# FNet mixing and one-token expert layer: stores moved from ScalarE to GpSimd, the sum behind the scores pushed ahead, and the second DFT of two pairs placed before the second group's sequence products

## The chip, the cores and the metric

The kernel runs on one core of a Trainium2 chip. The metric is the device time of one execution in microseconds. Five engines work side by side, each with its own queue of instructions in a fixed order: TensorE (PE in the profile; PEld is its loading of weights), VectorE (DVE), ScalarE (ACT), GpSimd (POOL) and SyncE (SP), which here only issues DMAs. An instruction at the head of a queue that waits holds everything behind it. ScalarE and GpSimd can issue DMAs, too, from the same queue in which their computing stands.

## The reference

With x of 2048 tokens by 576 features in fp32:

```python
a = einsum("bsd,ed->bse", LN(x), dft_hid_re)
b = einsum("bsd,ed->bse", LN(x), dft_hid_im)
h = x + einsum("ts,bse->bte", dft_seq_re, a) - einsum("ts,bse->bte", dft_seq_im, b)

n = LN(h)
r = n @ w_r                                  # one score per token
idx = argsort(-r)[:, :1]                     # the best token alone
g = silu(n[idx] @ w_gate); u = n[idx] @ w_up # 576 -> 4608
y = ((g * u) @ w_down) * sigmoid(r[idx])     # 4608 -> 576
out = h + n + scatter(y at idx)
```

All of the DFT matrices come as inputs, and so do the three weights of 4608 x 576, of which every byte is read for a single token.

## The kernel before

**Layout.** A token is p * 16 + k, with p the partition and k one of 16 slots, so X is a tile of 128 partitions by 16 rows of 576 features (and one column of padding). Slots k and 16 - k form a pair (1 to 7); 0 and 8 stand alone. In the code, `FOLDED` is the list of these nine, and `GROUPS` splits them into group 0 (pairs 1 to 5, ten rows of X) and group 1 (pairs 6 and 7, and 0 and 8, six rows).

**Stages.** The rows are loaded and folded by symmetry (`fold_d`, `fold`, `folded`) into XF. `seq(g, n)` are the products of the sequence matrix with XF for group g, five of them (n = 0 to 4) per group; `keep` copies their result out of PSUM, one half through ScalarE (L538) and one through VectorE (L542), into Z. `hid(g, c)` is the second DFT, over the features, of the c-th pair of group g: TensorE takes Z and the matrices WA, WB and WC (L569) and leaves `py`, to which VectorE adds the rows of X (`residual`, L577) and the totals (`totals`, L582). `seq` of group 1 overwrites nothing that `hid` of group 0 reads, but `keep` of group 1 writes into the same Z, and so waits for it.

**Scores, results, stores.** `spread_of` (ScalarE, L587) measures each row's variance, `root` (L221) takes the root of a batch (`BATCHES`: pairs 1 to 3, pairs 4 and 5, 6 and 7, then 0 and 8), `scores` (VectorE, L593 to 603) makes the scores R and the factors of a batch, `result` (ScalarE, L608) makes the output of one row in place, and `store` writes rows out: slots below 9 in runs (`STORE_RUNS`, (1, 3) is slots 1 to 3 in one DMA) from ScalarE's queue, the others by one indirect DMA each from GpSimd's. `scores` reads wsum, the sum of the router's weights, which `sum_wr` (L886, L887) makes from wr.

**Checks.** The kernel uses symmetries of the given matrices and proves them as it goes: mirrored blocks are fetched by indirect DMAs from GpSimd (`load_c` and `gather`, L278), VectorE subtracts or adds them (`off_s` L353, `off_t` L358, `off_h` L365, `off_w` L420 to 425) into one of two halves of Q, and ScalarE squares and sums these (L346). If the sum weren't zero a general program behind the kernel would run instead. The direct loads of the matrix are SP's (L335). A buffer of the matrix (D0, D1, D2 and seven raw ones) comes free when its checks and products are done.

**The token.** `argmax` finds the best score over all tokens (VectorE and TensorE in turn), `row_of_token` (L960) fetches its row of X, `to_all` (L966, L967) spreads it over the partitions, `normalized` (L974) writes it to PSUM as `xsp`, and `copy_xs` (ScalarE, L979) copies it to SBUF. The last three wait for all results.

**The expert layer.** The three weights come as 54 tiles of 576 KB by SP (`load_ffn`, L1052) into 33 places: whatever the stages before leave free (XF, Z, Q, WA, WB, WC, the D tiles and the raw ones), and each place again once its tile is used. Gate and up tiles are multiplied with the token's row and summed by VectorE (`products`, L1061, reading PSUM), or multiplied by GpSimd (L1072) or VectorE (L1068) and summed by ScalarE (L1077); `gated` (L1086 to 1089) makes H, `down` (L1097) multiplies with the down tiles on TensorE, and `last_store` (L1112) writes the token's row over what was stored.

**What sets the order.** Each step is entered with `add(engine, duration, function, *dependencies, tail=, push=)` into a `Plan`, and `Plan.order` lists them: engine by engine it takes, among the steps that are open at that time, the one with the largest remaining way to the end plus its push. That list is the order of the program, so each engine runs its steps in it. `EARLY` gives the spreads, roots, scores, results and stores of group 0 a push of 300. TensorE's steps are chained by `pe_last` in the order in which they are entered, so the loops that enter `seq_step` and `hid_step` write its order out by hand:

```python
for n in (0, 1):
    seq_step(1, n)
for c in range(len(GROUPS[0])):
    hid_step(0, c)
for n in (0, 1):
    keep_step(1, n)
for n in (2, 3, 4):
    seq_step(1, n)
```

The waits of the chip are set by what each instruction reads and writes, not by the plan; two engines that read the same PSUM tile also wait for each other in program order.

Of the kernel before, what the change touches and what calls it, by code (L numbers as in the profile page):

```python
# [16 lines left out]
D = 576  # L17
# [21 lines left out]
GROUPS = [[1, 2, 3, 4, 5], [6, 7, 0, 8]]  # L39
# [27 lines left out]
class Plan:  # L67
# [6 lines left out]
    def add(self, eng, dur, fn, *deps, tail=0.0, push=0.0):  # L74
        flat = []
        for d in deps:
            flat += d if isinstance(d, list) else [d]
        n = {"eng": eng, "dur": dur, "fn": fn, "deps": [d for d in flat if d], "tail": tail, "push": push}
        n["i"] = len(self.ops)
        self.ops.append(n)  # L80
        return n
# [54 lines left out]
def kernel(  # L136
# [13 lines left out]
    pe, act, dve, pool, sp = nc.tensor, nc.scalar, nc.vector, nc.gpsimd, nc.sync  # L150
# [121 lines left out]
    ov = out.rearrange("(p k) d -> p k d", k=NK)  # L272
# [9 lines left out]
    X = mp.tile([P, NK, XW], F32, name="X")  # L282
# [272 lines left out]
    def slots_of(j):  # L555
        return [j, NK - j] if j in PAIRS else [j]

    def cols(t, js):

        n0 = POS[js[0]]  # L560
        return t[:, n0 : n0 + sum(len(slots_of(j)) for j in js)]
# [49 lines left out]

    def store(k, m):
        if k < 9:
            st = act.dma_start(ov[:, k : k + m, :], X[:, k : k + m, 0:D])
        else:
            n = POS[k]
            st = pool.indirect_dma_start(  # L617
                out, bass.IndirectOffsetOnAxis(ap=ti[:, n : n + 1], axis=0), X[:, k, 0:D], None
            )

        for group in ("spread",) if k < 9 else ("spread", "direct"):
            tc.declare_no_dep(st.ins, group=group, reason="stores of different rows")
        tc.add_to_no_dep_group("direct" if k < 9 else "spread", st.ins)
        if k >= 9:
            pool.memset(tick, 0.0)

    tick = mp.tile([1, 1], F32, name="tick")
    junk2 = mp.tile([P, D], BF16, name="junk2")
# [3 lines left out]
    add = plan.add  # L632

    def then(f, *args):
        return lambda: f(*args)
# [20 lines left out]
    def in_turn(eng, f, mb, *deps):  # L656
        LAST[eng], d = load(eng, f, mb, LAST[eng], *deps)
        return d
# [11 lines left out]
    w0 = in_turn("SP", lambda: sp.dma_start(wr, w_r.unsqueeze(0).to_broadcast([P, D])), 0.295)  # L670
    MEAS, DOTX, DFOLD = {}, {}, {}
    for a, b in X_RUNS:
# [3 lines left out]
        m = [add("ACT", 0.95, then(measure, k), DFOLD[k]) for k in ks]  # L676
# [15 lines left out]
    for k in FOLDED:  # L692
        dg, use, at = [], [], []
        for sl in slots_of(k):
            n = next(places)
            UF[sl] = LATER[n]
            at.append(PLACE[n])
            if k in PAIRS:
                u, w = dgs.take()
# [50 lines left out]
    def c_half(j):  # L750
        u, w = qs.take()
        n = [add("DVE", 0.93, then(off_h, j, i, u), CU[j, i, False][1], w) for i in range(2)]
        for i in range(2):
            users[CU[j, i, False][0]].append(n[i])
        squares(u, 9 * P, n)

    def squares(u, w, n, ps=P):
        SQUARES.append(add("ACT", 0.3 + w / 1200, then(square, u, w, ps), n))
        qs.users[u].append(SQUARES[-1])
# [54 lines left out]
    RESULTS = []  # L814
# [28 lines left out]
    def hid_step(g, c):  # L843
        nonlocal pe_last
        j = GROUPS[g][c]
        (y0, w0_), (y1, w1_) = ys.take(), ys.take()
        pe_last = add("PE", 0.99, then(hid, g, c, [0]), KEPT[g], WRAP, w0_, w1_, pe_last)
        ZU.setdefault((g, False), []).append(pe_last)
        pe_last = add("PE", 4 * 0.99, then(hid, g, c, [1, 2, 3, 4]), pe_last)
        ZU.setdefault((g, True), []).append(pe_last)  # L850
        users["Z"] = [pe_last]
        for b in ("WA", "WB", "WC"):
            users[b] = [pe_last] + WS
        ks = slots_of(j)
        res = [add("DVE", 0.72, then(residual, j, k), pe_last, DOTX[k]) for k in ks]
        m = add("DVE", 0.2, then(totals, j), pe_last, [d for k in ks for d in DOTX[k]])
        ys.users[y0] += res + [m]
        ys.users[y1] += res + [m]
        RES[j] = [add("ACT", 0.9, then(spread_of, k), m, r, push=EARLY[g]) for k, r in zip(ks, res)]
        for js in BATCHES:  # L860
            if j == js[-1]:
                batch(js)

    def batch(js):
        push = EARLY[js[0] in GROUPS[1]]
        v = add(
            "ACT", 0.3, then(root, cols(SD, js), cols(VAR, js), UNIT), [n for j in js for n in RES[j]], push=push
        )
        f = add("DVE", 1.85, then(scores, js), v, ws, push=push)
        SCORES.append(f)  # L870
        for k in [k for j in js for k in slots_of(j)]:
            RESULTS.append(add("ACT", 0.86, then(result, k), f, push=push))
            if k > 8:
                o = add("POOL", 1.3, then(store, k, 1), RESULTS[-1], push=push)
                STORES.append(add("DMA", 0.8, None, o, tail=2.0, push=push))
        for k, n in STORE_RUNS:
            if k in js:
                o = add("ACT", 0.35, then(store, k, n), RESULTS, push=push)
                STORES.append(add("DMA", 0.76 * n, None, o, tail=2.0, push=push))

    EARLY = (300.0, 0.0)
# [4 lines left out]
        dve.tensor_reduce(wsum[:, 0:1], wr, axis=AX.X, op=OP.add)  # L886
        dve.tensor_scalar(wsum[:, 1:2], wsum[:, 0:1], -1.0 / D, None, op0=OP.mult)  # L887

    ws = add("DVE", 0.9, sum_wr, w0)
    def no_more(tag):  # L890
        for b in [b for b in free if type(b) is tuple and b[0] == tag]:
            free.remove(b)
# [23 lines left out]
            c_check(j, i)  # L916
    for j in GROUPS[1]:
        c_half(j)
    for n in (0, 1):
        seq_step(1, n)  # L920
    for c in range(len(GROUPS[0])):
        hid_step(0, c)
    for n in (0, 1):
        keep_step(1, n)
# [73 lines left out]
    xs_is = add("DVE", 1.2, normalized, step)  # L998
    xs_on = add("ACT", 0.7, copy_xs, xs_is)
# [23 lines left out]
    o = add("DVE", 1.0, check_sum, SCORES, SQUARES, xs_is)  # L1023
    o = add("PE", 0.3, check_all, o)
# [4 lines left out]
    for b in range(NJ // 4):  # L1029
        j = 4 * b  # L1030
# [92 lines left out]
    def plan_ffn(after):  # L1123

        del plan.ops[base[0] :]
        del moved[base[1] :]
        del in_flight["SP"][base[3] :]
        LAST["SP"], last = base[2], None
        plan.order()
        at = {b: over(ns) for b, ns in users.items()}  # L1130
        used = dict(users)
        came, done, where, got = {}, {}, {}, {}

        def load_to(n):

            while len(came) < min(n, len(FT)):
                b = min((b for b in at if used[b]), key=lambda b: at[b])
                w, j = FT[len(came)]
                w_, came[w, j] = load("SP", then(load_ffn, b, w, j), 0.59, used[b], LAST["SP"])
                LAST["SP"] = w_  # L1140
                used[b] = done[w, j] = []
                at[b] = after.get((w, j), 1e3 + len(came))

        def products_of(w, j):
            c = came[w, j]
            b = j // 4
            if j % 4 == 0 and b < 8 and (w == "u" or b % 2):
                o = add("POOL", 2.65, then(products_on_pool, w, j), c, xs_on)
                o = add("ACT", 1.75, then(sums, w, j), o)
            elif j % 4 == 0 and b < 8:  # L1150
                o = add("DVE", 1.36, then(products_only, w, j), c, xs_is)
                o = add("ACT", 1.75, then(sums, w, j), o)
            else:
                o = add("DVE", 1.68, then(products, w, j), c, xs_is)
            done[w, j].append(o)
            got[w, j] = o

        def gate_and_down(j0, j1):
            nonlocal last
            js = slice(j0, j1)  # L1160
            o = add("ACT", 0.3, then(gated, js, 0), [got["g", j] for j in range(j0, j1, JW)])
            o = add("DVE", 0.5, then(gated, js, 1), o, [got["u", j] for j in range(j0, j1, JW)])
            for j in range(j0, j1, JW):
                last = add("PE", 1.0, then(down, j), came["d", j], o, last)
                done["d", j].append(last)

        load_to(N_BUF)
        for b in range(NJ // 4):
            j = 4 * b
            if b < NJ // 4 - 1:  # L1170
                for w in "gu":
                    for r in (0, JW):
                        products_of(w, j + r)
                gate_and_down(j, j + 4)
            else:
                for r in (0, JW):
                    for w in "gu":
                        products_of(w, j + r)
                    gate_and_down(j + r, j + r + JW)
            load_to(N_BUF + 6 * (b + 1))  # L1180
        o = add("DVE", 0.8, last_of_row, last, row1)
        end = add("SP", 1.0, last_store, o, STORES, LAST["SP"])
        todo = plan.order()
        return end["end"], todo, {t: over(ns) for t, ns in done.items()}
# [14 lines left out]
    with tc.If(mv):  # L1199
        with ExitStack() as gen:  # L1200
# [29 lines left out]
            with ExitStack() as hs:  # L1230
# [4 lines left out]
                for k in range(NK):  # L1235
# [3 lines left out]
                    for a in range(5):  # L1239
                        w = min(P, D - a * P)  # L1240
# [3 lines left out]
                    for c in range(4):  # L1244
                        pa = zbank(f"gpa{k}_{c}")
                        for a in range(5):
                            w = min(P, D - a * P)
# [29 lines left out]
            c, ci = steps[4]()  # L1277
# [80 lines left out]
```

## Time and profile before

| | |
|---|---|
| median of 3 runs | 226.23 us (225.82 to 227.1) |
| profiled execution, device time | 224.98 us |
| profiled execution, span of the instructions | 223.3 us |
| mean granted TensorE clock | 0.855 |
| moved by DMA | 78.12 MB, 73.16 read and 4.72 written in HBM |
| busy: VectorE, ScalarE, TensorE, GpSimd | 178.4, 146.5, 135.7, 107.4 us |

Times in the profile are microseconds from the start of the span. A row of the timeline gives the start, the length, the engine, the line in the kernel, the operation, the tiles written and read with partitions x elements, and in brackets how long the engine had been idle before and what it waited for. A row of the waits reads: who waited <- for whom: us in total, times, the longest. A row of a page's groups ends in busy us, mean ns of one, and the idle time before. "SPq", "ACTq" are the queues in which DMAs are issued.

### The profile page before, as it was taken

Reading aid. Unit: us, or ns where it says so; the run is one execution under the profiler, and the core shown is the slowest. Engines: PE = TensorE matmul, PEld = TensorE weight load, DVE = VectorE, ACT = ScalarE, POOL = GpSimd, SP = SyncE. Lnnn points to the kernel's source line nnn. Section 1 sums busy time; section 2 is a strip of 40 time slices with the busy share of each in tenths; the row PEclk is TensorE's granted clock in tenths of the full one; section 3 lists DMA queues with packets and bytes.
Section 4 is the critical chain, followed back from the end, with each engine's and each line's share of the span. In section 5 each row is a group of like instructions: output and inputs, shape, how many; then the busy total and the mean of one; then the engine's idle time right before and its main releaser. Section 6 shows DMA issues by size and latency. Waiting matters only on the chain.

```text
span 223.3 us, 2563 instructions
## 1 busy us (share of the span) xinstructions
PE 135.7 (61%) x606; PEld 87.9 (39%) x606; DVE 178.4 (80%) x466; ACT 146.5 (66%) x288; POOL 107.4 (48%) x96
## 2 busy tenths in 40 slices
PE   0009879999900899999999999011400475565150
PEld 0006547755600687777876776000200121121010
DVE  6587988999999729799989999987415997978810
ACT  3386997599684077878558489999407898683000
POOL 7727897456468810258810000076005999990000
PEclk9999999999995699999999999655555599799755
DMA  6999999999899999799989999999999999999100
GB/s 213 385 360 410 414 415 404 397 334 375 306 385 415 373 410 348 226 339 277 365 365 330 376 421 357 376 376 417 419 414 419 420 420 410 413 412 411 70 9 5
DMA packets 19767, 78.12 MB, mean 350 GB/s; under 512 B 2460, under 2 KB 2462, under 8 KB 19745
## 3 DMA queue, kind: packets, MB, share of 16 engines
q1 hardware_dynamic: 14481, 55.09, 64.5%
q0 software_dynamic: 4032, 20.14, 23.9%
q10 hardware_dynamic: 1232, 2.65, 3.0%
q8 instruction: 6, 0.10, 0.2%
q14 instruction: 16, 0.13, 0.2%
HBM read 73.16 MB, written 4.72 MB: 349 GB/s over the span
## 4 chain that ended last, share of the span: by engine, by line
DMA 49%; PE 22%; DVE 13%; ACT 6%; issue 4%; SPq 2%; ACTq 0%; DVEq 0%
DMA D<-in_ct_dram 27%; PE py L569 11%; PE ps L524 10%; DMA out_dram<-X 8%; DMA WB<-in_wg_dram 5%; DMA D<-in_wg_dram 5%; DMA XF<-in_wd_dram 4%; DVE Q L353 4%; DVE junk L1061 3%; ACT X L608 3%; PE pd L1097 2%; DVE Q L358 2%; ACT Q L346 2%; SPq L305 2%; DVE X L577 1%
## 5 line engine op out<-in xcount | busy, mean ns | idle before, releaser
L346 ACT ACTIVATE Q<-Q 128x2944 bf16<-128x2944 bf16 (+4 forms) x30 | 56.3, 1877 | 13.9 <-DVE Q L358 5.1
L524 PE MATMUL ps<-D,XF 128*128 128x320 f32 (+3 forms) x216 | 46.5, 416 | 11.9 <-DMA D<-in_ct_dram 11.8
L524 PEld LDWEIGHTS ps<-D,XF 128*128 128x128 f32 (+1 forms) x216 | 33.2, 177 | 24.9 <-ACT Q L346 12.3
L278 POOL DMA_INDIRECT raw<-in_ct_dram,ic x21 | 27.4, 1304 | 17.4 <-DVE Q L353 13.6
L617 POOL DMA_INDIRECT out_dram<-X,ti x7 | 7.6, 1081 | 36.0 <-ACT X L608 33.4
L278 POOL DMA_INDIRECT D<-in_ct_dram,ic x11 | 15.4, 1403 | 14.5 <-DVE Q L358 11.6
L569 PE MATMUL py<-WA,Z 128*128 128x289 f32 (+1 forms) x72 | 20.7, 409 | 0.0
L569 PE MATMUL py<-WB,Z 128*128 128x289 f32 (+1 forms) x72 | 20.6, 408 | 0.0
L587 ACT ACTIVATE junk<-X,TD 128x576 bf16<-128x576 f32 x16 | 12.4, 773 | 5.8 <-DVE TD L582 5.6
L1097 PE MATMUL pd<-XF,H 128*1 128x288 f32 x32 | 5.9, 528 | 16.7 <-DVE H L1089 16.7
L365 DVE TENSOR_TENSOR Q<-D 128x320 bf16<-128x320 f32 (+1 forms) x36 | 14.5, 459 | 1.3 <-ACT Q L346 0.7
L569 PEld LDWEIGHTS py<-WA,Z 128*128 128x128 f32 x72 | 13.6, 189 | 4.2 <-DVE Q L358 0.4
L569 PEld LDWEIGHTS py<-WB,Z 128*128 128x128 f32 x72 | 13.6, 189 | 4.0
L496 PE MATMUL fo<-WB,diag 128*128 128x289 f32 (+1 forms) x8 | 4.2, 707 | 17.0 <-POOL diag L487 17.0
L487 POOL TENSOR_SCALAR diag<-ident,RX 128x128 f32<-128x128 f32 x14 | 11.4, 826 | 6.1 <-DVE RX L231 6.0
L469 ACT ACTIVATE junk<-X,XTD 128x576 bf16<-128x576 f32 x16 | 12.3, 771 | 2.0 <-DVE XTD L462 1.7
L358 DVE TENSOR_TENSOR Q<-raw,D 128x1152 bf16<-128x1152 f32 x10 | 13.5, 1351 | 0.0
L577 DVE TENSOR_TENSOR X<-py,X 128x576 f32<-128x576 f32 x16 | 11.4, 752 | 1.6 <-PE py L569 1.5
L608 ACT ACTIVATE X<-X,BB,UP 128x576 f32<-128x576 f32 x16 | 12.3, 857 | 0.0
L445 DVE SCALAR_TENSOR_TENSOR junk<-X,wr 128x576 bf16<-128x576 f32 x16 | 12.1, 758 | 0.2
L353 DVE TENSOR_TENSOR Q<-raw,D 128x896 bf16<-128x896 f32 x11 | 11.9, 1084 | 0.2 <-DMA D<-in_ct_dram 0.2
L1072 POOL TENSOR_TENSOR XF<-XF,Z 128x1152 f32<-128x1152 f32 x2 | 5.3, 2635 | 13.1 <-ACT Z L979 13.1
(220 smaller groups left out, 320.8 us busy)
## 6 DMA issues: line engine op xcount, KB each, us to landing
D<-in_ct_dram SPq DMA_DIRECT2D x22, 576.0 KB, 15.2
raw<-in_ct_dram SPq DMA_DIRECT2D x10, 576.0 KB, 9.2
D<-in_wg_dram SPq DMA_DIRECT2D x7, 576.0 KB, 11.4
f_u<-in_wu_dram SPq DMA_DIRECT2D x6, 576.0 KB, 11.3
D<-in_wd_dram SPq DMA_DIRECT2D x6, 576.0 KB, 9.7
f_g<-in_wg_dram SPq DMA_DIRECT2D x5, 576.0 KB, 9.6
D<-in_wu_dram SPq DMA_DIRECT2D x5, 576.0 KB, 8.7
XF<-in_wd_dram SPq DMA_DIRECT2D x4, 576.0 KB, 8.1
```

The source lines that it names most:

```text
L278: pool.indirect_dma_start(tile, None, view, bass.IndirectOffsetOnAxis(ap=rows, axis=0), element_offset=at)
L346: act.activation(t, t, AF.Square, accum_out=DS[0 : t.shape[0], n : n + 1])
L353: dve.tensor_tensor(o, C[j, i, True][:, 0:7, :], C[j, i, False][:, 7:0:-1, :], op=SIGN[i])
L358: dve.tensor_tensor(o, C[NK - j, i, False], C[j, i, False][:, :, ::-1], op=SIGN[i])
L365: dve.tensor_tensor(o[:, k::2, :], t[:, k::2, 0:HM], t[:, k::2, HM:P], op=op)
L445: dve.scalar_tensor_tensor(junk2[:, 0:D], X[:, k, 0:D], 1.0, wr, op0=OP.mult, op1=OP.mult, accum_out=XTD[:, n, 0:1])
L469: act.activation(junk[:, 0:D], X[:, k, 0:D], AF.Square, bias=XTD[:, n, 1:2], scale=-float(D), accum_out=VX[:, n : n + 1],)
L524: pe.matmul(cm(ZP[g, n][k % 2][p0 : p0 + m], w), XF[:, q, m0 : m0 + m], DT[g, i][:, :, k, 0:HM], start=k in (0, 1), stop=k in (6, 7),)
L569: pe.matmul(YP[GROUPS[g][c]][:, h, 0:w], Z[:, a, c * P : (c + 1) * P], w_block(a)[:, h * HD : h * HD + w], start=(a == 0), stop=(a == 4),)
L577: dve.tensor_tensor(t, y, t, op=OP.add)
L587: act.activation(junk[:, 0:D], X[:, k, 0:D], AF.Square, bias=TD[:, n, 1:2], scale=-float(D), accum_out=VAR[:, n : n + 1],)
L608: act.activation(t, t, AF.Identity, bias=BB[:, POS[k] : POS[k] + 1], scale=UP[:, POS[k] : POS[k] + 1])
```

## The change

It has four parts.

1. `store` issues the direct stores (slots below 9) from GpSimd instead of ScalarE, with a memset of one element behind each, which the indirect stores had already; in the plan they become steps of GpSimd of 1.3 instead of steps of ScalarE of 0.35.
2. The step `sum_wr` gets a push of 300.
3. `hid_step(0, 0)` and `hid_step(0, 1)` are entered before `seq_step(1, 0)` and `seq_step(1, 1)`; `hid_step(0, 2)` to `(0, 4)` stay behind them.
4. The products of the expert layer that VectorE makes depend, in the plan, on the copy of the token's row (`xs_on`) instead of the row in PSUM (`xs_is`).

```diff
     def store(k, m):
         if k < 9:
-            st = act.dma_start(ov[:, k : k + m, :], X[:, k : k + m, 0:D])
+            st = pool.dma_start(ov[:, k : k + m, :], X[:, k : k + m, 0:D])
...
         tc.add_to_no_dep_group("direct" if k < 9 else "spread", st.ins)
-        if k >= 9:
-            pool.memset(tick, 0.0)
+        pool.memset(tick, 0.0)
...
         for k, n in STORE_RUNS:
             if k in js:
-                o = add("ACT", 0.35, then(store, k, n), RESULTS, push=push)
+                o = add("POOL", 1.3, then(store, k, n), RESULTS, push=push)
                 STORES.append(add("DMA", 0.76 * n, None, o, tail=2.0, push=push))
...
-    ws = add("DVE", 0.9, sum_wr, w0)
+    ws = add("DVE", 0.9, sum_wr, w0, push=300.0)
...
     for j in GROUPS[1]:
         c_half(j)
+    for c in range(2):
+        hid_step(0, c)
     for n in (0, 1):
         seq_step(1, n)
-    for c in range(len(GROUPS[0])):
+    for c in range(2, len(GROUPS[0])):
         hid_step(0, c)
     for n in (0, 1):
         keep_step(1, n)
...
             elif j % 4 == 0 and b < 8:
-                o = add("DVE", 1.36, then(products_only, w, j), c, xs_is)
+                o = add("DVE", 1.36, then(products_only, w, j), c, xs_on)
                 o = add("ACT", 1.75, then(sums, w, j), o)
             else:
-                o = add("DVE", 1.68, then(products, w, j), c, xs_is)
+                o = add("DVE", 1.68, then(products, w, j), c, xs_on)
```

## The prediction

> **What bounds the kernel now.** I read the page first: its span, the rates in 40 slices (5.58 us each), and the chain that ended last.
>
> ```profile
> span 223.3 us, 2563 instructions
> GB/s 213 385 360 410 414 415 404 397 334 375 306 385 415 373 410 348 226 339 277 365 365 330 376 421 357 376 376 417 419 414 419 420 420 410 413 412 411 70 9 5
> DMA 49%; PE 22%; DVE 13%; ACT 6%; issue 4%; SPq 2%; ACTq 0%; DVEq 0%
> ```
>
> Half of the chain is DMA. The rates show two regimes: from slice 27 (150.7 us) to slice 36 (206.5 us) the DMA runs flat at 410 to 420 GB/s, while slices 15 to 26 wander between 226 and 421. The same by stage, from the view of windows (columns: window, its length, busy PE, PEld, DVE, ACT, POOL with instruction counts, granted clock, DMA share, GB/s):
>
> ```profile
> 73.00:83.00 10.00, 9.35 (x37) 8.04 (x38) 4.51 (x11) 3.70 (x4) 5.30 (x5) 0.82 1.02 389
> 83.00:95.00 12.00, 12.00 (x50) 9.27 (x49) 10.55 (x20) 9.64 (x14) 1.55 (x1) 1.00 0.87 295
> 95.00:107.00 12.00, 12.00 (x50) 9.28 (x49) 11.85 (x15) 8.99 (x14) 8.56 (x6) 1.00 0.94 312
> 107.00:119.00 12.00, 12.00 (x73) 9.48 (x73) 10.86 (x24) 7.06 (x13) 4.48 (x4) 1.00 0.92 343
> 119.00:131.00 12.00, 12.00 (x53) 9.04 (x50) 11.55 (x21) 8.07 (x12) 0.00 (x0) 1.00 1.02 389
> 131.00:143.00 12.00, 8.34 (x34) 6.07 (x33) 11.76 (x29) 10.95 (x19) 0.00 (x0) 0.94 0.99 373
> 143.00:150.00 7.00, 0.24 (x1) 0.28 (x2) 6.34 (x40) 6.97 (x12) 3.62 (x7) 0.50 1.02 386
> 168.00:204.00 36.00, 17.80 (x116) 5.43 (x118) 30.53 (x88) 28.50 (x77) 31.09 (x12) 0.80 1.03 415
> ```
>
> So the last quarter is a drain at 415 GB/s: it ends when the bytes end. Time can be gained where the DMA was underfed. Against 415, the six windows from 83 to 150 are short by 120x12, 103x12, 72x12, 26x12, 42x12 and 29x7 GB/s times us, that is 1.44 + 1.24 + 0.86 + 0.31 + 0.50 + 0.20 = 4.55 MB, or 11.0 us at 415; 3.54 MB of it, 8.5 us, lie before 119. No reordering of these loads and stores gains much more than 11 us.
>
> Why was it underfed, and what drains late? The chain in order of time, the timeline and the views of waits:
>
> ```profile
> 150.38 17.61 DMA out_dram<-X
> 169.00 0.66 ACT Z L979
> 193.26 11.39 DMA WB<-in_wg_dram
> 211.48 4.05 PE pd L1097 x16
> ```
>
> A store from ScalarE took 17.6 us, the ScalarE queue stood behind it, and only then came the copy of the routed token's row (L979) that the products wait for. From the last load on the chain (193.26 + 11.39 = 204.65) to the end lie products, 4.05 us of down matmuls and the last store: a tail of some 18 us that nothing in the change touches.
>
> **The change part by part.** *Early scores.* The scores of the first three pairs of rows need VAR (ready through the root L221) and wsum (L886).
>
> ```profile
> 102.25 0.30 ACT L221 ACTIVATE SD<-VAR,eps 128x6 f32<-128x6 f32 x1
> 140.83 0.74 DVE L886 TENSOR_REDUCE wsum<-wr 128x1 f32<-128x576 f32 x1
> 141.68 0.18 DVE L227 RECIPROCAL r0h<-SD 128x6 f32<-128x6 f32 x1
> L608 ACT ACTIVATE X<-X,BB,UP 128x576 f32<-128x576 f32 x16 | 12.3, 857 | 0.0
> out_dram<-X ACTq DMA_DIRECT2D x2, 288.0 KB, 7.0
> 145.31 1.25 POOL L617 DMA_INDIRECT out_dram<-X,ti  x1 [32.92 <-ACT X L608]
> L614 ACTq DMA_DIRECT2D out_dram<-X x5: 352/378/434, 147.3 to 168.5; - x5
> ```
>
> The root stood ready at 102.55; the scores, planned with the same push of 300, came 39 us later, because the sum of wr, with push 0, ran at 140.83. With the push on the sum, the scores of group 0 (pairs 1 to 5, ten rows of X) follow their roots, and so do their results and stores. One row of X is 288 KB = 0.295 MB, so ten are 2.95 MB, which move out of the drain (before, the first store of all was issued at 145.31, the five direct ones from 147.3 to 168.5) into the hole before 119, which has 3.54 MB. Worth: 2.95 / 0.415 = 7.1 us. This is the main term.
>
> Its cost: ten results of 0.857 us move to ScalarE before 119 (8.6 us; it had 24 + 12 - 9.64 - 8.99 - 7.06 = 10.3 us free in the three windows), and two scores of about 1.6 us (141.68 to 143.29 for the first) move to VectorE, 3.2 us. The sum itself goes early: 0.74 + 0.15 us of VectorE, bounded by 0 and 0.9 and taken at 0, since an idle of 5.45 us, shown next, lies behind it; without that cover it would be 0.9.
>
> *Second DFT of two pairs ahead.* TensorE in the timeline, and who stood behind it:
>
> ```profile
> 65.94 0.88 DVE L542 SCALAR_TENSOR_TENSOR Z<-ps,os 128x320 f32<-128x320 f32 x2
> 73.65 9.50 PE L524 MATMUL ps<-D,XF 128*128 128x256 f32 x36 [11.83 <-DMA D<-in_ct_dram]
> 79.30 0.47 ACT L538 ACTIVATE os<-ps,half 128x256 f32<-128x256 f32 x1 [6.35 <-PE ps L524]
> 79.68 2.65 ACT L346 ACTIVATE Q<-Q 128x2944 bf16<-128x2944 bf16 x1
> 82.45 0.76 DVE L420 TENSOR_TENSOR Q<-D,WB 128x576 bf16<-128x576 f32 x1 [5.45 <-ACT Q L346]
> 107.53 11.97 PE L524 MATMUL ps<-D,XF 128*128 128x256 f32 x72
> SPq L335 <- DVE Q L421: 10.3, 2, 8.6
> SPq L1052 <- PE ps L524: 12.6, 3, 11.7
> ```
>
> TensorE idles 11.83 us up to 73.65, waiting for the second group's matrix, while Z is complete at 66.8 and hid could run. From 73.65 it has no gap until hid ends (the windows show 12.00 of 12.00). Started at 66.85 with hid(0,0), the same stream ends 6.8 us earlier, if the second matrix half is there by 107.53 - 6.8 = 100.7. That frees XF 6.8 us earlier, for which SP waited up to 11.7 us. Also a jam dissolves: the copy L538 held ScalarE 6.35 us for the late matmuls, the square L346 behind it held a buffer of Q, VectorE stood 5.45 us and SP 8.6 us behind VectorE. In the new order that copy comes later in the plan, so I expect the 5.45 us back, less the 3.2 us of scores and what hid's residuals cost VectorE if hid starts cold: a net of -3 to +3 us on the checks.
>
> The clock: these 36 matmuls took 9.50 us and the 72 later ones 11.97, so a cold start cost 9.50 - 5.99 = 3.5 us. The idle before hid will still be 66.85 - 61.82 = 5.0 us, and I leave the 3.5 in. The Trainium skill (page "TensorE: Matmul & The Clock Gate", Part 1) says the gate falls to half after about 3.4 us of idle and needs about as long to open; by it the 3.5 us stay, too. If the clock survived, the stream would be 10.3 us early.
>
> How much supply this adds to the DMA is bounded by what the stores leave of the hole: 0 to 11.0 - 7.1 = 3.9 us. Against it stands crowding, next. I take the two as cancelling.
>
> *Stores from GpSimd.* Five direct stores leave the ScalarE queue, where they cost:
>
> ```profile
> ACT Z L979 <- issue: 9.9, 1, 9.9
> SPq L1052 <- DMA out_dram<-X: 13.2, 2, 12.9
> 156.83 0.52 DVE L960 TENSOR_SCALAR diag<-X,ghp 128x576 f32 x1 [1.19 <-ACT X L608]
> 169.68 0.76 DVE L1061 SCALAR_TENSOR_TENSOR junk<-XF,xsp 128x576 bf16<-128x576 f32 x1 [7.09 <-ACT Z L979]
> ```
>
> Gone: 5 x 0.378 us of issue on ScalarE and the 9.9 us before L979. The row of the token (L960) waits for all results; ten of sixteen, 8.6 us, are now done before. hid ended at 139.3 (8.34 us of TensorE after 131) and L979 began at 169.0, 29.7 us later; so it can begin at 139.3 - 6.8 + 29.7 - 9.9 - 8.6 = 143.7, 25 us early. But products wait for loads then: buffers come free sooner and the 7.09 us before L1061 go; for the end, in a drain set by bytes, I count 0. If the cover went, that is if buffers and not bytes paced the drain, it would gain, up to the 11.0. SP's wait of 12.9 us for a store falls in the flat part, so 0 too.
>
> Added: five SWDGE stores and five memsets of 0.09 us on GpSimd. No direct store from GpSimd is in the trace; the nearest rows are its indirect ones:
>
> ```profile
> L278 POOL DMA_INDIRECT raw<-in_ct_dram,ic x21 | 27.4, 1304 | 17.4 <-DVE Q L353 13.6
> L617 POOL DMA_INDIRECT out_dram<-X,ti x7 | 7.6, 1081 | 36.0 <-ACT X L608 33.4
> 104.81 3.75 POOL L278 DMA_INDIRECT D<-in_ct_dram,ic  x1 [0.30 <-issue]
> 91.12 1.55 POOL L278 DMA_INDIRECT D<-in_ct_dram,ic  x1 [11.60 <-DVE Q L358]
> ```
>
> Between 1.08 (L617) and 3.75 us each, 5.4 to 18.8 us in all; a saving below the ScalarE issue is excluded, since GpSimd computes these. I take 1.3, as for L278, 6.5 us. GpSimd has room (1.55 of 12 us busy in 83 to 95, 0.00 from 119 to 143), but the queue matters: a store waits there for ScalarE's result with mirrored gathers behind it, and for these VectorE's checks (L353) and SP wait. Crowding therefore costs 0 to 5 us of checks.
>
> A rule speaks against this edit: the Trainium skill ("SBUF — State Buffer", section "SBUF: two separate sides") says that some VectorE modes lock GpSimd out while it writes descriptors, and to issue from ScalarE or SP instead. Beside a VectorE busy 11.85 of 12 us the issues here took 1.08 and 1.30 us in the mean, and one 3.75, which may be this; by the rule the sum would have the high end, 18.8 us. The sum goes by the rows.
>
> *Products after the copy (xs_on).* VectorE's products stand behind 0.66 us of L979. L1061 waited for L979 already; cost 0 to 0.66, hidden by loads, taken at 0.
>
> **Sum.** 7.1 us off: profiled execution 224.98 (span 223.3 and 1.7 around it) to 217.9; the median of the runs shown is 226.23, 1.25 higher, so 226.23 - 7.1 = **219.1 us**.
>
> **The rivals.**
> *A: ScalarE becomes the bound.* In 83 to 107 it is busy 18.6 of 24 us; six results (5.1) bring it to 23.7, and VectorE is at 22.4 + 1.6. Squares then come late and VectorE waits for Q. For it: both at the brim; against it: the jam at 79 is gone. Price: the checks end about 3.1 us later (8.6 less the 5.45 of idle), so 4.0 us are gained: 222.2.
> *B: the hole is filled wholly,* as stream and jam supply the loads: 226.23 - 11.0 = 215.2. Against it: checks hardly get earlier.
> *C, slower: stores block the gathers on GpSimd.* Up to four issues (three indirect, one direct) among the gathers at 91 to 112, at 3.75 us 15.0, plus six rows, 1.77 MB, of stores ahead of them in the software queue, 4.3 us: 19.3, less 3.4 us of GpSimd idle in 95 to 107 and the 5.45 of VectorE: checks and later loads 10.4 us late, less 7.1 gained: 229.5. It turns slower once gathers slip more than 7.1 us net. For it: one 3.75 in the trace; against it: all others near 1.3.
> *D: it doesn't do what it says.* The scores are planned late all the same, the drain stays: within 0 to 1 us of 226.2. Against it: root and scores have the same push and the root ran at 102.
>
> **How the numbers follow.** Forecast 0.60, A 0.17, B 0.08, C 0.07, D 0.08. A measurement of this kernel can tell about 0.5%, 1.1 us, from no change. Faster by over 0.5% (below 225.1): forecast, A and B, 0.85; within: D, 0.08; slower: C, 0.07. The range holds forecast, A and B: low 226.23 - 11.0 - 0.6 (26 GB/s short over 73 to 83) = 214.6; high 225.0, just under D; 0.15 are left out.
>
> **What would show it.** Scores on VectorE and the first L608 near 95 to 105 instead of 141; L614's stores on GpSimd at 95 to 120; 83 to 119 above 370 GB/s; hid starting near 67 and the last hid ending near 132; no 5.45 us wait at L420; L979 between 144 and 150; drain at 415 ending near 197.5. Wrong if gathers (L278) wait behind stores, if VectorE idles for L346 over 3 us in 83 to 119, or if the flat part falls below 400 GB/s.

## The result, and the profile after

| | before | after |
|---|---|---|
| median, same chip | 226.66 us (225.82 to 230.19) | 220.19 us (219.63 to 220.77) |
| ratio, 95% interval | | 0.9733 [0.9684, 0.9783] |
| profiled execution: device time, span | 224.98, 223.3 us | 219.63, 217.9 us |

The change gains 2.7%. Ratios here and below leave out executions that ran over 1.5% above the fastest of their kernel, while a median over all executions can contain some. The predicted 219.1 us lies 1.1 us, 0.5%, below the median. The size of the gain was right (7.1 us predicted, 6.5 measured by the medians, 5.4 by the two profiled executions; the profiled execution of before lies 1.7 us under its median, so gains read from its profile come out small). Its main reason was not right, as the experiments show.

The page of the kernel after: its span, the rates in 40 slices (5.45 us each now), and the shares of the chain that ended last.

```profile
span 217.9 us, 2566 instructions
GB/s 185 369 399 406 414 405 414 410 323 397 312 386 275 352 391 405 396 417 301 326 409 423 413 421 417 413 415 422 416 411 411 412 414 410 414 412 386 23 8 5
DMA 38%; DVE 36%; issue 9%; PE 6%; POOL 5%; ACT 3%; DVEq 0%; POOLq 0%; SPq 0%; ACTq 0%
```

The flat part begins at slice 20 (109 us) instead of slice 27 (150.7 us), with one low slice, 12 (275 GB/s), that wasn't there before. VectorE, 13% of the chain before, is now 36%. The windows of the kernel after (columns as in the prediction: window, length, busy PE, PEld, DVE, ACT, POOL, granted clock, DMA share, GB/s):

```profile
67.00:73.00 6.00, 6.00 (x26) 4.57 (x25) 5.93 (x11) 4.51 (x5) 5.08 (x4) 1.00 0.87 279
73.00:83.00 10.00, 10.00 (x47) 8.51 (x46) 10.00 (x19) 9.11 (x13) 8.17 (x7) 1.00 1.03 379
83.00:95.00 12.00, 12.00 (x50) 8.90 (x48) 12.00 (x20) 9.51 (x16) 9.34 (x4) 1.00 1.01 402
95.00:107.00 12.00, 10.93 (x64) 8.58 (x64) 11.76 (x29) 10.61 (x13) 10.04 (x12) 1.00 0.95 325
107.00:119.00 12.00, 11.44 (x54) 8.19 (x51) 11.44 (x32) 8.89 (x16) 6.37 (x7) 1.00 1.02 415
119.00:131.00 12.00, 10.06 (x40) 7.48 (x40) 11.97 (x16) 11.72 (x19) 2.10 (x6) 1.00 1.02 416
131.00:143.00 12.00, 0.77 (x2) 0.50 (x2) 11.26 (x44) 11.04 (x19) 2.00 (x4) 0.52 1.02 414
143.00:150.00 7.00, 3.06 (x6) 1.68 (x6) 4.59 (x22) 4.01 (x6) 2.50 (x7) 0.50 1.02 417
0.00:150.00 150.00, 111.62 (x460) 81.09 (x460) 136.93 (x351) 116.05 (x208) 81.51 (x94) 0.93 0.99 378
60.00:131.00 71.00, 67.42 (x299) 51.43 (x297) 70.06 (x131) 56.94 (x81) 41.80 (x36) 1.00 1.00 378
```

Compare with the prediction's rows of before. From 83 to 95 the rate went from 295 to 402, from 107 to 119 from 343 to 415; the hole from 95 to 107 stayed (312 and 325). And VectorE is busy 10.00 of 10 and 12.00 of 12 us where it was 4.51 and 10.55. The last two rows, over longer stretches, read as follows in the kernel before:

```profile
0.00:150.00 150.00, 108.22 (x453) 79.14 (x454) 131.69 (x327) 108.60 (x196) 71.75 (x77) 0.94 0.97 361
60.00:131.00 71.00, 59.17 (x262) 46.05 (x261) 62.18 (x107) 46.51 (x66) 29.56 (x22) 0.93 0.96 353
```

By 150 us into the span the kernel after has moved (378 - 361) x 150 = 2.55 MB more, which is 6.1 us at 415 GB/s; the span is 5.4 us shorter. In the same time VectorE got 136.93 - 131.69 = 5.2 us more work done. Both sums are about as large as the gain. The question of the experiments is which part of the change brings them about. In the timeline of after:

```profile
62.55 1.15 PE L569 MATMUL py<-WA,Z 128*128 128x289 f32 x4
66.91 1.21 POOL L278 DMA_INDIRECT wAm<-in_wt_dram,iw  x1 [6.30 <-DVE Q L358]
72.36 7.99 PE L524 MATMUL ps<-D,XF 128*128 128x256 f32 x36
97.26 4.65 ACT L608 ACTIVATE X<-X,BB,UP 128x576 f32<-128x576 f32 x6
105.42 0.33 SPq L1053 DMA_DIRECT2D XF<-in_wg_dram  x1
105.62 0.83 POOL L614 DMA_DIRECT2D out_dram<-X  x1
127.92 1.14 PE L569 MATMUL py<-WC,Z 128*128 128x289 f32 x4
145.90 2.96 SPq L1053 DMA_DIRECT2D D<-in_wg_dram  x2
151.42 0.65 ACT L980 ACTIVATE Z<-xsp 128x576 f32<-128x576 f32 x1 [1.13 <-DVE sq L1008]
```

TensorE goes from the first group's products to hid at 62.55 without a pause, results and direct stores of group 0 run from 97 and 105, the XF places are loaded at 105.42 instead of 116.50, and the token's row is copied at 151.42 instead of 169.00. Near the new low slice GpSimd waits 6.30 us, to 66.91, for a check on VectorE (L358) that now stands behind other work. That wait alone doesn't make the slice low: in `u_pool`, a run shown below, it is 6.20 us, and 67 to 73 runs at 362 GB/s instead of 279. The chain of after in order of time ends so:

```profile
138.77 15.10 DMA f_g<-in_wg_dram
...
188.09 11.37 DMA f_g<-in_wg_dram
...
206.15 4.06 PE pd L1098 x16
```

From 53.63 to 138.77 the chain runs mostly over VectorE's checks and its other work, then over one load after another to 199.46, 5.2 us earlier than before (204.65), and then over the same tail of 18 us.

### The profile page after: what moved, and what is told of

Read it like the earlier page. It is cut to its first block, busy times and chain, and to the rows that moved or that the text cites. A ratio compares the mean times of both kernels' runs of the same rounds, so it can differ in the third digit from the quotient of the medians.

```text
span 217.9 us, 2566 instructions
## 1 busy us (share of the span) xinstructions
PE 139.5 (64%) x606; PEld 88.6 (41%) x606; DVE 178.0 (82%) x466; ACT 145.2 (67%) x288; POOL 112.8 (52%) x106
## 4 chain that ended last, share of the span: by engine, by line
DMA 38%; DVE 36%; issue 9%; PE 6%; POOL 5%; ACT 3%; DVEq 0%; POOLq 0%; SPq 0%; ACTq 0%
DMA f_g<-in_wg_dram 12%; DVE Q L353 10%; DMA D<-in_ct_dram 7%; DMA XF<-in_wd_dram 5%; DVE Q L358 5%; DMA D<-in_wg_dram 5%; DMA D<-in_wu_dram 5%; DVE X L577 4%; DMA X<-in_x_dram,ti 3%; PE fo L496 3%; DVE Z L542 3%; DVE junk L445 3%; DVE junk L1062 3%; PE pd L1098 2%; POOL diag L487 2%
## 5 line engine op out<-in xcount | busy, mean ns | idle before, releaser
L346 ACT ACTIVATE Q<-Q 128x2944 bf16<-128x2944 bf16 (+4 forms) x30 | 56.2, 1876 | 12.4 <-DVE Q L353 4.6
L524 PE MATMUL ps<-D,XF 128*128 128x320 f32 (+3 forms) x216 | 44.8, 408 | 1.1 <-DMA D<-in_ct_dram 1.1
L524 PEld LDWEIGHTS ps<-D,XF 128*128 128x128 f32 (+1 forms) x216 | 32.1, 172 | 13.4 <-issue 3.0
L278 POOL DMA_INDIRECT raw<-in_ct_dram,ic x21 | 29.3, 1394 | 14.2 <-DVE Q L353 9.7
L278 POOL DMA_INDIRECT D<-in_ct_dram,ic x11 | 17.0, 1543 | 5.8 <-DVE Q L358 2.1
L1098 PE MATMUL pd<-XF,H 128*1 128x288 f32 x32 | 7.9, 673 | 10.4 <-DVE H L1090 10.4
L487 POOL TENSOR_SCALAR diag<-ident,RX 128x128 f32<-128x128 f32 x14 | 9.9, 721 | 7.5 <-DVE RX L231 7.2
L358 DVE TENSOR_TENSOR Q<-raw,D 128x1152 bf16<-128x1152 f32 x10 | 13.5, 1350 | 0.0
L1098 PE MATMUL pd<-D,H 128*1 128x288 f32 x40 | 6.3, 459 | 10.6 <-DVE H L1090 10.6
L1073 POOL TENSOR_TENSOR D<-D,Z 128x1152 f32<-128x1152 f32 x4 | 10.5, 2623 | 3.8 <-DMA D<-in_wg_dram 3.8
```

Of the source, the lines that this page charges most:

```text
L278: pool.indirect_dma_start(tile, None, view, bass.IndirectOffsetOnAxis(ap=rows, axis=0), element_offset=at)
L346: act.activation(t, t, AF.Square, accum_out=DS[0 : t.shape[0], n : n + 1])
L358: dve.tensor_tensor(o, C[NK - j, i, False], C[j, i, False][:, :, ::-1], op=SIGN[i])
L487: pool.tensor_scalar(t, ident, RX[:, n : n + 1], None, op0=OP.mult)
L524: pe.matmul(cm(ZP[g, n][k % 2][p0 : p0 + m], w), XF[:, q, m0 : m0 + m], DT[g, i][:, :, k, 0:HM], start=k in (0, 1), stop=k in (6, 7),)
L1098: pe.matmul(T["pd"][h][at(h), :HD], H[:, j : j + 1], WB["d", j0][:, r, half(h)], start=(j == 0), stop=(j == NJ - 1),)
```

## The experiments

The theory under test was the prediction's: the drain ends when its bytes end, and early scores move 2.95 MB of stores out of it (7.1 us). Its rival was that the second DFT ahead of the second group's products supplies the loads earlier, whatever the stores do. Each ratio is against runs of the kernel before on the same chip.

### Each part of the change alone

`p_sum` is the kernel before with part 2 alone, `p_hid` with part 3 alone, `p_pool` with part 1 alone. Part 4 was not run by itself.

```diff
-    ws = add("DVE", 0.9, sum_wr, w0)
+    ws = add("DVE", 0.9, sum_wr, w0, push=300.0)     # p_sum
```

```diff
+    for c in range(2):                               # p_hid
+        hid_step(0, c)
     for n in (0, 1):
         seq_step(1, n)
-    for c in range(len(GROUPS[0])):
+    for c in range(2, len(GROUPS[0])):
```

```diff
-            st = act.dma_start(ov[:, k : k + m, :], X[:, k : k + m, 0:D])
+            st = pool.dma_start(ov[:, k : k + m, :], X[:, k : k + m, 0:D])   # p_pool
```

> Before, with the push on the sum of wr alone (direct stores still on ScalarE, second DFT in the old order). Theory of the bytes (the prediction's): group 0's ten rows, 2.95 MB, leave the drain for the hole ahead of 119, so about 7.1 us faster, near 219.5; less, 221 to 223, if ScalarE's queue stands behind its own stores among the checks. Rival of the supply (the gain comes from the second DFT started early, which frees XF and dissolves the jam at 79): within 1 us of before. Rival of the queue (the gain comes from ScalarE's queue and SP no longer waiting for direct stores): within 1 us of before.

> Before, with the second DFT of two pairs placed ahead, alone. Theory of the bytes: what the earlier stream adds to the supply, 0 to 3.9 us faster, likely about 1, since the stores stay in the drain. Rival of the supply: 5 us or more faster. Rival of the queue: within 1 us of before.

> Before, with the direct stores on GpSimd alone. Theory of the bytes: all stores are still issued after 140 and lie in the drain; the copy of the token's row comes some 8 to 10 us earlier, and the end stays within 1 us of before. Rival of the supply: the same. Rival of the queue: 4 to 7 us faster.

| | median, us | ratio, 95% interval |
|---|---|---|
| p_sum | 225.80 | 0.9946 [0.9910, 0.9981] |
| p_hid | 223.57 | 0.9788 [0.9666, 0.9910] |
| p_pool | 227.22 | 0.9928 [0.9885, 0.9971] |

The early scores alone, which were to bring nearly all, bring half a per cent, and the stores on GpSimd alone 0.7%, which its median over all executions (227.22, before on that chip 226.73) doesn't bear out. The DFT alone brings 2.1%, with an interval from 0.9 to 3.3%. Windows of p_sum:

```profile
83.00:95.00 12.00, 12.00 (x52) 9.49 (x51) 9.79 (x18) 9.62 (x14) 1.55 (x1) 1.00 0.83 288
95.00:107.00 12.00, 12.00 (x51) 9.25 (x50) 10.91 (x25) 8.76 (x14) 4.25 (x4) 1.00 0.77 265
119.00:131.00 12.00, 12.00 (x64) 8.77 (x61) 11.36 (x28) 9.82 (x17) 0.36 (x2) 1.00 1.03 420
131.00:143.00 12.00, 10.65 (x43) 7.61 (x41) 11.93 (x20) 10.11 (x16) 2.38 (x4) 1.00 1.02 415
```

The stores do run early there, between 108 and 133, and fill 119 to 143 (420 and 415 against 389 and 373). But the hole ahead of them got deeper, 265 against 312 in 95 to 107: stores can't fill it, since they come only after it. What came later is in p_sum's timeline, with one row of the chain of before ahead of it:

```profile
60.10 13.20 DMA D<-in_ct_dram
...
75.83 9.47 PE L524 MATMUL ps<-D,XF 128*128 128x256 f32 x36 [9.26 <-DMA D<-in_ct_dram]
84.59 0.76 DVE L420 TENSOR_TENSOR Q<-D,WB 128x576 bf16<-128x576 f32 x1 [6.80 <-ACT Q L346]
109.68 11.97 PE L524 MATMUL ps<-D,XF 128*128 128x256 f32 x72
```

The first products of the second group begin 2.18 us later than before (75.83 against 73.65), because the load they wait for began at 61.17 instead of 60.10 and took 14.30 us instead of 13.20. The later ones follow 2.15 us late (109.68 against 107.53), and VectorE's wait at L420 has grown from 5.45 to 6.80 us. The push changed the planner's list on VectorE as well: copies out of PSUM (L542) stand at other places between the checks. Whether that list or the chance of one execution made the load late isn't shown. Still, a kernel of one part isn't that part and nothing else: the planner writes a new order for all engines each time.

### The stores of group 0 held back

In the kernel after, the ten rows of group 0 are stored late, all else as it is. `late_stores` plans them behind the scores of group 1, `late2` behind the first store of group 1 on GpSimd.

```diff
-            if k > 8:                                          # late2
+            if k > 8 and js[0] in GROUPS[0]:
+                held.append((k, 1))
+            elif k > 8:
                 o = add("POOL", 1.3, then(store, k, 1), RESULTS[-1], push=push)
...
+                while held:
+                    k0, n = held.pop(0)
+                    o = add("POOL", 1.3, then(store, k0, n), o, push=300.0)
```

> After, but the stores of group 0's ten rows are issued only behind the scores of pairs 6 and 7, near 137; scores and results stay early. Theory of the bytes: the 2.95 MB are back in the drain, about 7.1 us slower than after, near 227. Rivals of the supply and of the queue: within 1 us of after, near 220.

> After, but all stores of group 0's ten rows stand behind the first store of group 1 in GpSimd's queue, so that none is issued before about 141; scores and results stay early. Theory of the bytes: 2.95 MB go back into the drain, 7.1 us slower than after, near 227. Theory of the supply, now the favourite (loads are there to be issued from about 107 on whenever the checks and TensorE release places early, and stores and loads only take each other's turn): within 1.5 us of after, near 220.

`late_stores`: 219.48 us, 0.9662 [0.9590, 0.9733]. It decides nothing: its trace has the 864 KB store still at 109.77, and only three single rows moved. `late2` does what it says, no store before 140.93, and gives 220.85 us, 0.9714 [0.9676, 0.9753]: not to be told from the kernel after by these intervals, where the theory demanded the whole gain back. (Other variants with early stores lie at 0.9662 to 0.9677, so a loss of half a per cent, some 1 us, is possible.) Late2 in the views of windows and timeline:

```profile
119.00:131.00 12.00, 10.01 (x40) 7.42 (x40) 11.96 (x16) 11.75 (x19) 0.00 (x0) 1.00 0.99 381
131.00:143.00 12.00, 0.77 (x2) 0.50 (x2) 11.27 (x45) 11.04 (x19) 1.84 (x3) 0.50 1.01 397
0.00:150.00 150.00, 111.16 (x460) 80.92 (x460) 136.85 (x352) 116.33 (x209) 78.15 (x85) 0.93 0.99 373
```

```profile
140.47 1.77 SPq L1063 DMA_DIRECT2D D<-in_wg_dram  x2
140.93 1.20 POOL L617 DMA_INDIRECT out_dram<-X,ti  x1 [31.39 <-ACT X L608]
146.01 0.83 POOL L614 DMA_DIRECT2D out_dram<-X  x1
```

Without stores in the way, SP runs ahead with loads: the pair of D loads that the kernel after issues at 145.90 is issued at 140.47, and four more tiles, 2.36 MB, follow by 150. Loads took the room of the stores. Not wholly: 119 to 143 runs at 381 and 397 instead of 416 and 414, and by 150 (378 - 373) x 150 = 0.75 MB less has moved, 1.8 us at 415. That is the most that these two traces allow the early stores beside the DFT ahead; the measured times don't tell it from nothing.

### Each part taken out of the change

`u_hid` is the kernel after without part 3, `u_sum` without part 2, `u_pool` with the direct stores back on ScalarE: the edits above, reversed.

> After without the second DFT ahead (old order on TensorE), with the push on the sum, the stores on GpSimd and the products behind the copy. Theory of the supply: most of the gain goes, 4 to 6 us slower than after, 224 to 226. Theory of the bytes: the stores still lie in the hole, within 2 us of after.

> After without the push on the sum, so scores, results and stores of group 0 are late again, in the drain. Theory of the supply: 0 to 2 us slower than after, 220 to 222. Theory of the bytes: 5 to 7 us slower, 225 to 227.

> After with the direct stores back on ScalarE's queue. Theory of the supply: the places come free as in after, within 1.5 us of it: 219 to 222. Rival of the queue: ScalarE and SP stand behind stores again, 3 us or more slower.

| | median, us | ratio, 95% interval |
|---|---|---|
| u_hid | 227.67 | 1.0020 [0.9982, 1.0058] |
| u_sum | 224.58 | 0.9852 [0.9796, 0.9908] |
| u_pool | 219.88 | 0.9666 [0.9615, 0.9718] |

Without the DFT ahead nothing is left of the gain, though parts 1, 2 and 4 are all in and the stores of group 0 run nearly as early as in p_sum (from 109.95 us, 108.18 there). Without the push on the sum over half is left, 3.4 us by the ratio (2.1 to 4.6). The engine that issues the stores makes no difference. Windows and timeline of u_hid:

```profile
83.00:95.00 12.00, 12.00 (x53) 9.68 (x52) 8.35 (x16) 9.92 (x13) 0.00 (x0) 1.00 0.86 305
95.00:107.00 12.00, 12.00 (x50) 9.27 (x49) 10.59 (x23) 8.27 (x14) 4.34 (x4) 1.00 0.67 229
119.00:131.00 12.00, 12.00 (x69) 8.48 (x68) 10.39 (x29) 8.26 (x15) 2.46 (x3) 1.00 1.02 416
```

```profile
76.12 10.94 PE L524 MATMUL ps<-D,XF 128*128 128x256 f32 x36 [9.04 <-DMA D<-in_ct_dram]
86.35 0.76 DVE L420 TENSOR_TENSOR Q<-D,WB 128x576 bf16<-128x576 f32 x1 [7.73 <-ACT Q L346]
```

The early part is the one that lacks: 229 GB/s in 95 to 107, GpSimd without a gather in 83 to 95, TensorE dry for 9.04 us, to 76.12, and VectorE standing for 7.73 us behind it.

### One pair ahead, or all five

`hid1` and `hid5` are the kernel after with one and with five pairs ahead of the second group's products.

```diff
-    for c in range(2):
+    for c in range(5):          # hid5; range(1) in hid1
         hid_step(0, c)
```

> After with one pair's second DFT ahead instead of two. TensorE then runs dry again, some 5 us, until the second group's matrix is there near 73, and may start cold. Theory of the supply: XF, Z and the W places come free 5 to 8 us later than in after, 2 to 5 us are lost: 222 to 225. If any earlier second DFT does: within 1 us of after.

> After with all five pairs' second DFT ahead. TensorE doesn't run dry either, and its stream ends at about the same time; theory of the supply: within 1.5 us of after, near 220. Rival: what counts is when the first two sequence products of group 1 run, or the residuals crowd VectorE ahead of its checks: 2 to 4 us slower.

hid1: 223.15 us, 0.9768 [0.9705, 0.9832]. hid5: 220.17 us, 0.9677 [0.9627, 0.9727]. Two pairs are enough. Whether one is less can't be told: its interval overlaps that of the kernel after, and the execution that was profiled (224.85 us) is its slowest.

### ScalarE's jam taken away alone

The prediction laid the 5.45 us of VectorE before L420 to ScalarE's copy L538, which waits for the late products with the square L346 behind it. `unjam` is the kernel before with only that copy, for the first two products of group 1, planned behind the second DFT of pair 2.

```diff
     for n in (0, 1):
-        keep_step(1, n)
+        keep_step(1, n, ZU[0, True][1])
```

> Before, with one thing changed: ScalarE's copies of the second group's first two products (L538) stand in its queue behind the second DFT of pair 2, so they no longer hold the squares (L346) up; the order of TensorE, the sum and the stores are those of before. If the jam is what the second DFT's new place dissolves: VectorE's wait of 5.45 us at L420 goes, SP goes on 5 us earlier, and most of the 3.2 us that p_hid gained comes, 2 to 4 us. If TensorE's own earlier stream (XF free early) is what counts: within 1 us of before.

227.07 us, 0.9993 [0.9958, 1.0028]: nothing. Windows and timeline of unjam:

```profile
73.00:83.00 10.00, 8.69 (x31) 7.37 (x32) 9.97 (x23) 7.79 (x8) 7.08 (x6) 0.72 1.03 374
83.00:95.00 12.00, 12.00 (x51) 9.40 (x50) 5.49 (x8) 5.71 (x8) 1.55 (x1) 1.00 0.86 331
```

```profile
89.33 1.42 DVE L577 TENSOR_TENSOR X<-py,X 128x576 f32<-128x576 f32 x2 [5.35 <-PE py L569]
```

VectorE no longer stands in 73 to 83 (9.97 of 10 us), but in 83 to 95 (5.49 of 12): the same five microseconds, at the next place in its queue that needs TensorE, eleven instructions behind L420. There it adds the first product of hid. What VectorE's queue waited for was TensorE, here dry for 10.53 us until 74.31; ScalarE was only the messenger.

### The early XF places closed again

`xf_late` is the kernel after in which the XF tiles count as free 20 us later in the plan of the loads, so that SP fills them behind two other places.

```diff
-        at = {b: over(ns) for b, ns in users.items()}
+        at = {b: over(ns) + 20.0 * (b[0] == "XF") for b, ns in users.items()}
```

> After, but SP takes the five places in XF for weights only behind the first two raw places, so some 12 us later (near 118 instead of 105); the order of TensorE, VectorE and ScalarE ahead of the weights, the sum and the stores stay. If it is the early release of XF that feeds the DMA: a hole of some 10 us opens at 107 to 118, of which stores fill a part, and 4 to 7 us are lost: 224 to 227. If the second DFT's new place helps by something else (checks, scores, the token's row early): within 1.5 us of after, near 220.

220.11 us, 0.9671 [0.9618, 0.9723]: no loss. In the timeline of xf_late SP takes f_g and f_u first, and XF at 116.51:

```profile
114.37 0.33 SPq L1053 DMA_DIRECT2D f_g<-in_wg_dram  x1
...
116.51 0.34 SPq L1053 DMA_DIRECT2D XF<-in_wu_dram  x1
```

So XF alone isn't the cause either. But its windows show 410 GB/s in 107 to 119 without those loads: the stores of group 0 are there. Stores cover for XF here as loads covered for the stores in late2; a kernel with both held back was not tried.

### What separates the kernels

VectorE's busy time and the rate from the view of windows, in the order of the span (one profiled execution each; the one of before lies under its median, and u_sum, hid1 and p_pool stand behind the table, as theirs were 0.9 to 1.7 us slower than their medians):

| | VectorE busy of the 71 us from 60 to 131 | GB/s, 0 to 150 | span, us |
|---|---|---|---|
| u_hid | 59.27 | 354 | 226.2 |
| unjam | 62.57 | 359 | 225.1 |
| p_sum | 61.24 | 359 | 224.3 |
| before | 62.18 | 361 | 223.3 |
| p_hid | 66.68 | 367 | 221.6 |
| late2 | 69.79 | 373 | 219.1 |
| xf_late | 70.03 | 376 | 218.7 |
| hid5 | 69.78 | 376 | 218.5 |
| u_pool | 70.09 | 376 | 218.5 |
| after | 70.06 | 378 | 217.9 |
| late_stores | 70.03 | 378 | 217.7 |

The same three numbers are 65.39, 361, 224.2 for u_sum, 63.60, 363, 223.2 for hid1 and 60.83, 357, 226.3 for p_pool.

From first to last, 24 GB/s over 150 us are 3.6 MB, 8.7 us at 415, and the spans differ by 8.5 us: the drain does end when its bytes end, in every one of these kernels. And over these 150 us the rate follows VectorE, though not window by window: 95 to 107 of the kernel after has 325 GB/s with VectorE busy 11.76 of 12 us. Where VectorE stands for 8 to 12 of these 71 us, nothing is gained; where it stands for about one, the whole gain is there, whether the stores are early or late, on GpSimd or ScalarE, and whether XF is filled early. VectorE's checks bring the places free and let GpSimd's gathers go, so while it stands the DMA can have too little to do.

That is a regularity over eleven kernels and not a proof. TensorE's busy time from 60 to 131 parts them almost as well: 59.2 to 60.9 us in the first four, 66.5 to 67.9 in the others, p_hid (66.50) among them. Busy time up to a fixed moment also grows when loads come earlier, so it can be effect as well as cause. No run stopped VectorE in the kernel after and changed nothing else, and single executions differ by more than a microsecond before the change can act: the same load of SP stands at 58.15 us in the kernel after and at 59.45 in xf_late, which differs from it only behind 102 us.

## Why the prediction was right in time and wrong in its main reason

**The drain set by bytes: right.** See the table above. The last load landed at 199.46 (predicted 197.5), and the tail stayed at 18 us.

**7.1 us for stores moved out of the drain: wrong.** This was the step that failed: late2 bounds it by 0 to 1.8 us. That the forecast came within 1.1 us is luck: a term of 7.1 us was too large by at least 5.3, and another that was taken at nothing made up for it. Two things were overlooked. Group 0's stores start at 101 to 105, and so the deepest part of the hole (83 to 107) is ahead of them. And with TensorE early, SP has loads ready for the room from 107 on: stores and loads were taken as adding up, and they stand in for each other.

**Supply from TensorE's earlier stream, 0 to 3.9 us, cancelled against crowding: wrong in size, and it is the main term.** Its upper bound was what the stores would leave of the hole. Without it (u_hid) the sum and the stores bring nothing; with it and without the push (u_sum) 3.4 us are there. With the stores at 0 to 1.8 us, at least 4.3 of the 6.1 us of bytes come by another way than stores, from the stream alone or from the stream together with the early scores. Crowding didn't show: in the kernel after VectorE has no wait between 64 and 111 us.

**The wait of 5.45 us before L420: gone as predicted, for another reason.** Unjam shows that the jam on ScalarE wasn't its cause but passed on TensorE's dry spell. The 5.45 us were netted against scores and residuals (-3 to +3 us); VectorE in fact won 70.06 - 62.18 = 7.9 us of busy time by 131.

**hid at 66.85, cold, the stream 6.8 us early: too careful.** On VectorE the copy into Z comes earlier, hid starts at 62.55 right behind the products, the granted clock in 67 to 73 is 1.00 (0.50 before), and the 36 products take 7.99 us instead of 9.50. The last hid ends at 127.92 + 1.14 = 129.06, before at 139.3: 10.3 us earlier. The prediction gave this number for a clock that survives, but by other terms, so the agreement is chance. The stream began 73.65 - 62.55 = 11.1 us earlier and took 0.8 us longer. And the 3.5 us for a cold start were misread: of the 72 products that took 11.97 us in the kernel before, 36 are of half the size (128\*64, 4.1 us together in the view of groups with the shapes kept apart), and the 36 of the full shape took 7.9 us at a clock of 1.00. So the cold start cost 9.50 - 7.9 = 1.6 us, not 3.5. The idle of 5.0 us that the 3.5 stood for didn't come.

**Stores from GpSimd at 0: right** (u_pool). The five stores took 0.57 to 0.83 us each, below the lower bound of 1.08 and the 1.3 that was taken. The rule of the Trainium skill ("SBUF — State Buffer", section "SBUF: two separate sides") that speaks against issuing from GpSimd cost nothing that these runs show: two gathers took 3.63 us in the kernel after, and with the stores back on ScalarE (u_pool) the same two took 3.62 and 3.63.

**The token's copy between 144 and 150, worth 0 for the end: right in its worth.** It ran at 151.42, 1.4 us behind the stretch forecast. In p_hid it ran at 161.80, and the DMA still moved 417 GB/s from 150 to 168.

**The rivals.** The time lies nearest to the forecast. B was the one that let the stream feed the hole, on top of the stores, at 215.2: too fast, since the hole in 95 to 107 stayed and a new one opened at 67 to 73 (279 GB/s, 0.8 MB, 2.0 us). A and C didn't occur.

**What stays open** is how the push on the sum adds its 1.2%, 2.7 us (u_sum 0.9852, after 0.9733, intervals just apart). Late2 leaves the early stores up to 1.8 us of it by bytes and nothing by the ratios. p_hid and late2, neither with a store before 140.9, differ in the scores (and in parts 1 and 4) and moved nearly the same from 60 to 131, but VectorE was busy 66.68 and 69.79 us there. The first three rows are p_hid, the last is late2:

```profile
60.00:131.00 71.00, 66.50 (x296) 51.00 (x294) 66.68 (x107) 49.47 (x71) 28.15 (x22) 1.00 0.98 373
119.00:131.00 12.00, 11.23 (x47) 8.29 (x45) 12.00 (x15) 9.97 (x18) 0.00 (x0) 1.00 0.95 371
131.00:143.00 12.00, 0.30 (x2) 0.00 (x0) 11.29 (x49) 10.89 (x19) 1.82 (x3) 0.67 0.99 381
...
60.00:131.00 71.00, 67.33 (x298) 51.46 (x297) 69.79 (x131) 57.01 (x80) 33.76 (x22) 1.00 0.99 374
```

Around 85 to 88 late2 has no wait on VectorE, and p_hid has two, of 1.33 and 1.78 us. What p_hid lacks against the kernel after shows mostly behind 119: 371 and 381 GB/s to 143, against 416 and 414. Late2 has 381 and 397 there and so lacks part of the same. No run settles how much of this is VectorE's and how much the stores'.

## What to carry to other kernels

When the DMA has holes in the middle and a full drain at the end, bytes that move into a hole count only if nothing else would have filled it. To find out, hold them back in the finished kernel and see whether the time returns. A wait is to be followed through the queue to the engine that has nothing to do; taking away the messenger (unjam) moves the wait to the next place in the queue that needs the same engine. Work that is ready belongs in front of work whose operands are still on their way, above all on the engine for whose results all others queue.

## What the runs showed of the hardware that was not expected

A direct store issued from GpSimd is cheap here: 0.83 us for three rows (864 KB), 0.57 us for the smallest, beside 0.35 to 0.43 us from ScalarE's queue for the same stores (u_pool) and about 1.1 us for an indirect one.

How long TensorE may idle before its clock is lower shows on the same 36 products. Behind 3.59 us of idle they took 8.01 us in p_hid, with a granted clock of 1.00 in 73 to 83; behind 4.44 us they took 9.54 in u_sum, and behind 9.04 to 11.83 us they took 9.47 to 10.94 in u_hid, p_sum, unjam and the kernel before (one execution each). What lies between 3.59 and 4.44 us no run here shows.

```profile
75.49 8.01 PE L524 MATMUL ps<-D,XF 128*128 128x256 f32 x36 [3.59 <-DMA wAm<-in_wt_dram,iw]
```
